# Twenty input loads on ScalarE's queue, w of eight chunks as 64 partitions, transposes by DMA, and a new order

## The chip, the cores and the metric

The kernel runs on one core of a Trainium2 chip. The metric is the device time of one execution in microseconds (us); less is better. Engines are named as in the profile: PE (TensorE), DVE (VectorE), ACT (ScalarE), POOL (GpSimd), SP (SyncE, which here only issues transfers).

## The reference

Two layers in sequence: a recurrent attention with a decaying state, and a gated long convolution.

```python
# r, k, v, w: (4, 8, 768, 48); u: (8, 48)
for t in range(S):
    cur = einsum('bhd,bhe->bhde', u[None] * k[:, :, t], v[:, :, t])
    y[:, :, t] = einsum('bhd,bhde->bhe', r[:, :, t], state + cur)
    state = w[:, :, t, :, None] * state + einsum('bhd,bhe->bhde', k[:, :, t], v[:, :, t])
x = y.transpose(0, 2, 1, 3).reshape(4, 768, 384)
x1, x2, x3 = split(x @ w_proj, 3)                       # w_proj: (384, 1152)
conv = irfft(rfft(x2, axis=1) * rfft(filter_fft, axis=0))  # circular, over 768 steps
out = (x1 * conv * x3) @ w_out                          # (4, 768, 384), float32
```

## The kernel before

**Attention.** The 768 steps of each of 4 batches are cut into 6 chunks of 128, 24 chunks in all (0 to 23). Loads and some elementwise work go by groups of one or two chunks: [0], [1], [2, 3], [4, 5], then pairs. For a chunk i:

- `lw`, `lk`, `lr`, `lv` load 128 tokens x 8 heads x 48 values, one token to a partition. A token's 48 floats of one head lie together in memory, so a packet has 192 bytes (line 1313).
- `ln` takes the logarithm of w; `cs` sums it over time on PE with two triangular masks (lines 1347, 1348) and, in single columns, over the chunk (1350); `ex` takes the exponential on ACT within PSUM (1353); `kq` multiplies it with k and r on DVE (1356); `ph` is the decay of the whole chunk.
- `tr` turns the result on PE, eight 128x128 blocks (1368), and `qk` copies it out of PSUM. `sc` makes the scores (1380), `mt` and `mc` mask them: DVE multiplies with a mask (1396), or ACT copies and POOL cuts (1401).
- `ki`, `kv`, `su` update the state; `yi`, `ys`, `y` make the chunk's output in PSUM; `xn` copies it out, `yt` turns three blocks (1482), `xT` copies them out.
- `rk`, `ru`, `rh`, `cc`, `vc` are the term with u, `vb` is v in bf16.

**Second layer,** for a batch once its chunks are there: `p`, `q`, `xw` are projections (1624, 1661), `cp` and `cxw` copy them out, `cq` multiplies two of them (1649). `sd` folds x2 in time, `f` is the forward transform (1511), `u` and `p` (on DVE) multiply with the filter's spectrum, `E` is the inverse transform (1716). In it the even half is copied out (`cE`), and `aE` add and subtract the odd half (1738, 1742). An `E` marked `Q` in the order works on half the columns, and `dE` make the two halves of the result from it (1751); the others need no `dE`. `yE` multiplies with the gate, `o` is the last projection (1780), `co` copies it out and `so` stores it (1796).

**What sets the order.** Nothing is scheduled at run time. A list of some 1,100 lines, `ORDER`, gives each operation its engine (P, D, A, G or S; M, N, C, Q, V, X are variants of an operation; `-` leaves it out) and, for PE, a PSUM bank; each engine executes its own operations in the list's order and waits by semaphore for what they need. `warm n bank` are n filler matmuls without use (1259). All input loads are issued by SP in the list's order. Input buffers are rotated: w has 3 buffers of a group each, k with r and v have 4, outputs 5 (`NLW, NLD, NO`).

Of the kernel before, what the change touches and what calls it, by code (L numbers as in the profile page):

```python
# [9 lines left out]
FP32 = mybir.dt.float32  # L10
# [28 lines left out]
NLW, NLD, NG, NF, NS, NX, NO = 3, 4, 3, 4, 3, 3, 5  # L39
# [5 lines left out]
warm 16 0  # L45
pads D
smalls D
zeros D
lw0 S
first A  # L50
ln0 A
imaps G
maske G smalls
maps G smalls
ang2 D
ang1 D
lw3 S
lw2 S
lr0 S
lk0 S  # L60
kz2 G
maskn G
cs0 P 4
kz0 G
ln2 A
u S
signs D
maski G
ia1.0 G
ex0 A  # L70
kq0 D
ia2.0 D
warm 9 1
cs3 P 6
kz3 G zeros
cs2 P 2
ur A
warm 5 1
um P 0
rk0 G  # L80
ub A
lv0 S
lw1 S
lr3 S
lk1 S
tr0 P 1
qk0 D
ph0 A
vb0 A
ex3 A  # L90
ln1 A
ang0 D
ru0 G ia2.0
rh0 G kq0
cc0 D
kz1 D
vc0 D
warm 6 0
sc0 P 0
warm 2 4  # L100
cs1 P 4
mt0.1 -
mt0.0 N
kv0 P 0
ex2 A
ex1 A
ia0.0 G zeros
su0 D
mc0.0 C cc0
lk3 S  # L110
lr1 S
mc0.1 -
warm 4 1
yi0 P 0
kq3 D
y0 P
xn0 A
tr3 P 1
kq1 D
lk2 S  # L120
lr2 S
lv1 S
lw4 S
lw5 S
tr1 P 0
rk1 G
ru1 D
rh1 G ru1
ph1 A
qk3 D  # L130
xa0 -
ph3 A
kq2 D
lv2 S
lv3 S
yt0 P 6
sc3 P 4
xT0 A
mt3.0 M
qk1 A  # L140
vb1 A
ph2 A
warm 4 7
tr2 P 6
lr4 S
lk4 S
ki1 P 1
sc1 P 2
qk2 A
mc3.0 -  # L150
mt1.1 -
kv1 P
warm 2 7
sc2 P 6
cc1 D
rk2 G
lk5 S
ru2 D
ia2.1 G
vc1 G  # L160
mc1.1 -
mt1.0 M
mc1.0 -
mt2.1 -
mt3.1 -
lr5 S
ln3 A
warm 5 0
cs4 P 4
yi1 P 2  # L170
rh2 G ru2
su1 D
vb2 G ru2
ys1 P
mc2.1 -
lv5 S
lv4 S
cc2 D
vc2 G cc2
mt2.0 M  # L180
wproj1 G mt2.0
ki2 P 0
y1 P
lw6 S
warm 5 1
kv2 P
xn1 A
ex4 A
cs5 P 2
xa1 -  # L190
mc2.0 -
yt1 P 1
su2 D
ki3 P 0
kv3 P
yi2 P 6
ys2 P
y2 P
mc3.1 -
xT1 A  # L200
kq4 D
tr4 P 1
ex5 A
ph4 A
wproj0 G su2
kq5 D
su3 D
xn2 A
yi3 P 4
ys3 P  # L210
qk4 A
y3 P
rk3 G
xn3 D
warm 4 6
tr5 P 6
qk5 D
xa2 -
ph5 A
yt2 P 2  # L220
lw7 S
xa3 -
yt3 P 7
xT3 D
xT2 D
ki4 P 5
warm 4 1
sc5 P 6
trig A
sin0 A  # L230
sin2 A
vb3 G xn3
mt5.1 -
mc5.1 -
ia1.1 G xT2
kv4 P
sc4 P 3
ia0.1 G xT2
mt4.0 N
ru3 D  # L240
rh3 D
cc3 D
vc3 G cc3
warm 7 1
xw0.2 P 0
is A
mt5.0 M
su4 D
mt4.1 -
xw0.0 P 2  # L250
mc5.0 -
mc4.0 C
yi5 P 6
cxw0.2 D
yi4 P 4
cxw0.0 D
lk7 S
sin1 A
table A
ln4 A  # L260
lr7 S
mc4.1 -
ys5 P
ys4 P
y5 P
xn5 D
y4 P
xn4 D
p0.0.0 P 0
lk6 S  # L270
xa4 -
xa5 -
yt5 P 6
p0.2.0 P 3
lr6 S
rk4 G xn5
xT5 D
yt4 P 2
cs7 P 6
cp0.0.0 D  # L280
filt S
cp0.2.0 D
cs6 P 4
xT4 A
xw0.4 P 0
ex7 A
kq7 D
lv7 S
ex6 A
kq6 D  # L290
cxw0.4 A
if3 A
p0.0.1 P 2
tr7 P 1
ph7 A
cp0.0.1 A
tr6 P 6
qk6 A
qk7 A
sd0.0.0 D  # L300
ru4 D
lw8 S
lw9 S
p0.2.1 P 0
ph6 A
warm 4 7
f0.0 P 2
lv6 S
cp0.2.1 A
cf0.0 A  # L310
sd0.1.0 D
f0.2 P 5
sc7 P 0
mt7.1 -
rh4 D
fsd0 D
fsd1 D
lk8 S
lr9 S
cf0.2 A  # L320
warm 5 7
sc6 P 6
lr8 S
mt7.0 N
mt6.1 -
warm 6 4
h1 P 1
mt6.0 M
ln5 A
cc4 D  # L330
h2 P 4
mc6.0 -
mc7.1 -
lk9 S
mc7.0 C rh4
hc1 A
hg1 D
vb4 G
vc4 G fsd1
lv8 S  # L340
lv9 S
mc6.1 -
lk11 S
hc2 A
h0 P 6
hg2 D
kv6 P 3
su6 D
lk10 S
lw10 S  # L350
lr10 S
hc0 A
cs8 P 0
wproj2 G
warm 2 2
yi6 P 4
y6 P
lw11 S
hg0 D
ex8 A  # L360
xn6 A
xa6 -
yi7 P 2
ys7 P
y7 P
xn7 A
xa7 -
cs9 P 4
kq8 D
lr11 S  # L370
ex9 A
yt6 P 3
yt7 P 7
xT7 D
kq9 D
xT6 A
ki7 P 2
kv7 P
tr8 P 6
qk8 D  # L380
ph8 A
rk5 G cc4
ru5 G
vb5 A
lv11 S
xw1.0 P 0
lr12 S
lv10 S
tr9 P 3
sc8 P 6  # L390
if2 A
ph9 A
lw12 S
rh5 D
cc5 D
lk12 S
lw13 S
lv13 S
cxw1.0 A
qk9 A  # L400
lv12 S
mt8.1 -
su7 D
lk13 S
mt8.0 M
vc5 G cc5
lk15 S
f0.1 P 4
q0.2.0 P 3
ki8 P 2  # L410
cq0.2.0 D
mc8.1 -
sc9 P 0
lr13 S
cf0.1 A
mt9.0 N
mc9.0 C
if1 A
kv8 P
q0.0.1 P 6  # L420
q0.2.1 P 3
yi8 P 4
ln6 A
u10.0 D
mt9.1 -
su8 D
cq0.0.1 D
mc8.0 -
u00.0 D
yi9 P 1  # L430
lw15 S
# [3 lines left out]
lk14 S  # L435
mc9.1 -
xn8 A
lw14 S
lr14 S
xa8 -  # L440
y9 P
lr15 S
q0.0.0 P 6
lv15 S
yt8 P 0
cs10 P 4
if0 A
xn9 A
xa9 -
ki9 P 2  # L450
yt9 P 1
lk17 S
cq0.0.0 D
lv14 S
xT8 A
ex10 A
xT9 A
kv9 P
lw17 S
cs11 P 6  # L460
ex11 A
p1.2.0 P 0
cq0.2.1 D
rk6 G cq0.0.1
cp1.2.0 A
su9 D
lv17 S
ru6 D
xw1.2 P 1
kq10 D  # L470
tr10 P 3
kq11 D
rh6 G ru6
ph10 A
cxw1.2 A
p1.0.0 P 4
cc6 D
p0.0 D
ph11 A
qk10 A  # L480
cp1.0.0 A
ln7 A
tr11 P 7
vb6 G
vc6 G
q1.0.0 P 1
qk11 D
sc10 P 3
sc11 P 6
q1.2.0 P 5  # L490
lr17 S
lw16 S
ki10 P 0
mt10.1 A
cq1.0.0 D
cs12 P 1
mt10.0 D
lk16 S
yi10 - 3
ys10 P  # L500
mt11.1 -
mc11.1 -
mc10.0 -
mc10.1 G
y10 P
mt11.0 N
cs13 P 6
kv10 P
cq1.2.0 D
ex12 A  # L510
xn10 V
kq12 D
vb7 G
ex13 A
E0.0 P 4
mc11.0 C mt10.0
ph12 A
yi11 - 1
cE0.0 A
su10 D  # L520
kq13 D
ph13 A
tr12 P 3
ys11 P
kv12 P 0
aE0.0.0 D
rk7 G
ru7 G
xa10 -
qk12 A  # L530
y11 P
E0.1 P 6
xn11 V
xa11 -
su12 D
cE0.1 A
aE0.0.1 D
dE0.0.0 -
rh7 G aE0.0.0
yt11 P 1  # L540
xT11 D
yt10 P 0
ki13 P 3
tr13 P 2
E0.2 P 4
kv13 P
aE0.1.1 D
aE0.1.0 D
xT10 A
qk13 D  # L550
ln8 A
cE0.2 A
sc12 P 6
lk18 S
lr16 S
mt12.1 -
su13 D
aE0.2.1 D
aE0.2.0 D
mt12.0 N  # L560
sc13 P 0
p1.0.1 P 2
mt13.1 D
mt13.0 D
lv16 S
cp1.0.1 A
cs14 P 6
ex14 A
dE0.1.0 -
xw1.4 P 4  # L570
q1.0.1 P 1
cc7 D
kq14 D
cq1.0.1 D
p1.2.1 P 3
vb8 A
cxw1.4 A
rk8 G
# [240 lines left out]
ex22 A
# [1059 lines left out]
```

## Time and profile before

| | |
|---|---|
| median of 3 runs | 155.38 us (154.06 to 155.63) |
| profiled execution | 153.79 us |
| its span, first to last instruction | 152.1 us |
| busy: PE, DVE, ACT, POOL | 142.4, 135.6, 123.1, 96.1 us |
| input loads by SP | 96, of 192 KB each |
| packets, bytes of the hardware queue | 102,498, 24.78 MB |
| filler matmuls | 90 |
| granted TensorE clock | 1.000 |

The profile is of one execution. An engine's busy time is the union of its instructions' times; the rows of single instructions overlap by some tens of nanoseconds, so that the rows of an engine sum to more. A stretch of time can be cut out and each engine's busy time read in it. "Idle before" names what ended an engine's wait. The chain of waits goes back from the last instruction, at each step to what released it.

### The profile page before, as it was taken

The page shows a single profiled execution, that of the slowest core. Times are in us where ns is not written, and L with a number is a line of the kernel's source. Part 1 is how long each engine was busy: PE and PEld are TensorE (multiplying, and loading weights), DVE is VectorE, ACT ScalarE, POOL GpSimd, SP SyncE. Part 2 cuts the span into 40 slices and gives each one's busy share as a digit, 9 for nine tenths or more (in the row PEclk, how much of TensorE's full clock was granted, in tenths as well). Part 3 has the DMA queues.
Part 4 walks back from the last instruction along what each step waited for, and adds up shares of the span by engine and source line. Part 5 has one row for each costly group of instructions (what it writes and reads, how often), then busy time and mean ns, then how long its engine had stood idle before and what let it go on. Part 6 is the DMA issues. An engine that isn't in the chain of part 4 may idle for free.

```text
span 152.1 us, 4409 instructions
## 1 busy us (share of the span) xinstructions
PE 142.4 (94%) x1725; PEld 95.3 (63%) x1725; DVE 135.6 (89%) x252; ACT 123.1 (81%) x204; POOL 96.1 (63%) x101
## 2 busy tenths in 40 slices
PE   7986999999999999999999999999999999999980
PEld 5654667666556657567666776576687666656530
DVE  3589996989969999999989999999999999999950
ACT  4576849989979989997889899979999987576370
POOL 6577989944069567888968974885299164830310
PEclk9999999999999999999999999999999999999999
DMA  4999899999999999989899899998940000002956
GB/s 97 216 214 223 163 221 174 203 182 272 250 209 170 197 172 219 212 162 218 170 203 218 160 203 192 198 213 169 324 133 0 4 0 0 4 0 88 395 210 240
DMA packets 104118, 26.23 MB, mean 172 GB/s; under 512 B 100129, under 2 KB 102690, under 8 KB 104098
## 3 DMA queue, kind: packets, MB, share of 16 engines
q1 hardware_dynamic: 102498, 24.78, 74.2%
q0 software_dynamic: 1600, 1.18, 5.6%
q8 instruction: 13, 0.21, 0.5%
q14 instruction: 7, 0.06, 0.1%
HBM read 22.41 MB, written 4.72 MB: 178 GB/s over the span
## 4 chain that ended last, share of the span: by engine, by line
PE 42%; DVE 15%; DMA 13%; SPq 10%; ACT 8%; issue 5%; POOL 4%; POOLq 1%; DVEq 0%; ACTq 0%
SPq L1313 10%; PE banks L1624 7%; PE banks L1511 6%; PE banks L1780 5%; DMA w<-in_w_dram 5%; PE banks L1661 3%; PE banks L1368 3%; PE banks L1380 3%; DMA v<-in_v_dram 3%; DMA kr<-in_r_dram 3%; DVE kq L1356 3%; PE banks L1458 3%; DMA kr<-in_k_dram 2%; ACT banks L1353 2%; PE banks L1716 2%
## 5 line engine op out<-in xcount | busy, mean ns | idle before, releaser
L1209 POOL TENSOR_TENSOR rk<-kr 128x768 bf16<-128x768 f32 (+1 forms) x13 | 23.0, 1766 | 9.5 <-DMA kr<-in_r_dram 5.9
L1624 PE MATMUL banks<-xT,wproj 128*128 128x384 bf16 x144 | 27.9, 326 | 0.2 <-ACT x L1213 0.2
L1356 DVE TENSOR_TENSOR kq<-banks,kr 128x768 bf16<-128x768 f32 x24 | 22.4, 949 | 3.6 <-DMA kr<-in_k_dram 1.7
L1401 POOL TENSOR_SCALAR_AFFINE_SELECT mt<-mt 128x512 bf16<-128x512 bf16 (+1 forms) x15 | 14.0, 940 | 12.7 <-ACT mt L1213 8.6
L1209 POOL TENSOR_TENSOR vc<-vb,cc 128x768 bf16<-128x768 bf16 (+1 forms) x11 | 17.4, 1577 | 5.1 <-DVE cc L1332 3.3
L1353 ACT ACTIVATE banks<-banks 128x768 f32<-128x768 f32 x24 | 19.1, 806 | 0.5 <-PE banks L1350 0.2
L1624 PEld LDWEIGHTS <-wproj 128*128 128x128 bf16 x144 | 13.0, 97 | 8.1 <-issue 0.7
L1213 ACT ACTIVATE x<-banks 128x768 bf16<-128x768 f32 (+1 forms) x24 | 16.8, 709 | 1.6 <-PE banks L1661 1.1
L1396 DVE TENSOR_TENSOR mt<-banks,mask_excl 128x1024 bf16<-128x1024 f32 (+1 forms) x17 | 16.2, 965 | 0.2 <-PE banks L1380 0.2
L1213 ACT ACTIVATE qk<-banks 128x1024 bf16<-128x1024 bf16 x16 | 16.2, 1029 | 0.0
L1368 PE MATMUL banks<-ident,kq 128*128 128x128 bf16 x192 | 14.3, 219 | 1.4 <-ACT xn L1213 0.6
L1259 PE MATMUL banks<-wt 128*128 128x256 bf16 x90 | 14.4, 300 | 1.1 <-DVE wt L1282 1.1
L1368 PEld LDWEIGHTS <-kq 128*128 128x128 bf16 x192 | 11.8, 97 | 4.2 <-DVE kq L1356 1.6
L1780 PE MATMUL banks<-wout,y 128*128 128x384 bf16 x72 | 13.3, 326 | 0.5 <-DVE g L1649 0.3
L1661 PE MATMUL banks<-wproj,xT 128*128 128x384 bf16 x72 | 13.6, 325 | 0.0
L1511 PE MATMUL banks<-sd,F 128*128 128x384 bf16 (+1 forms) x96 | 13.4, 328 | 0.2 <-ACT phi L1360 0.2
L1319 ACT ACTIVATE lg<-w 128x768 bf16<-128x768 f32 (+1 forms) x13 | 10.4, 799 | 3.4 <-DMA w<-in_w_dram 3.4
L1213 ACT ACTIVATE mt<-banks 128x512 bf16<-128x512 f32 (+1 forms) x15 | 11.6, 802 | 1.1 <-PE banks L1380 0.7
L1213 ACT ACTIVATE o<-banks 128x768 f32<-128x768 f32 (+1 forms) x12 | 9.3, 785 | 3.5 <-PE banks L1780 3.4
L1511 PEld LDWEIGHTS <-F 128*128 128x128 bf16 (+1 forms) x120 | 8.5, 103 | 5.8 <-issue 1.1
L1649 DVE TENSOR_TENSOR g<-banks,x 128x384 bf16<-128x384 f32 (+1 forms) x16 | 11.8, 748 | 0.3 <-PE banks L1624 0.2
L1209 DVE TENSOR_TENSOR U<-X,hh 128x2304 bf16<-128x2304 bf16 (+1 forms) x12 | 11.9, 1022 | 0.0
(109 smaller groups left out, 331.1 us busy)
## 6 DMA issues: line engine op xcount, KB each, us to landing
w<-in_w_dram SPq DMA_DIRECT2D x24, 192.0 KB, 4.4
kr<-in_r_dram SPq DMA_DIRECT2D x24, 192.0 KB, 3.9
kr<-in_k_dram SPq DMA_DIRECT2D x24, 192.0 KB, 3.8
v<-in_v_dram SPq DMA_DIRECT2D x24, 192.0 KB, 3.9
out_dram<-o SPq DMA_DIRECT2D x11, 384.0 KB, 4.0
U<-in_moe_filter_fft_dram SPq DMA_DIRECT2D x1, 1152.0 KB, 7.3
wproj<-in_moe_w_proj_dram POOLq DMA_DIRECT2D x3, 288.0 KB, 5.9
out_dram<-o SPq DMA_DIRECT2D x2, 192.0 KB, 2.2
```

What stands on the lines that cost most here:

```text
L1209: return eng(e).tensor_mul(o, a, b)
L1213: return nc.scalar.activation(out=o, in_=a, func=AF.Copy)
L1259: nc.tensor.matmul(banks[:, at, 0:256], wt[:, 0:L], wt, start=True, stop=True)
L1313: op(f"l{name}{i}", [SP], lambda e, bk, t=t, x=x, q=q, rw=rw: nc.sync.dma_start(out=t[:, q], in_=x[b, :, rw, :].rearrange("h t d -> t h d" ...
L1353: op(f"ex{i}", [ACT], lambda e, bk: nc.scalar.activation(out=two(bk, f"cs{i}")[:, :, 0:C], in_=two(bk, f"cs{i}")[:, :, 0:C], func=AF.Exp), ...
L1356: op(f"kq{i}", [DVE], lambda e, bk: nc.vector.tensor_mul(kq[f][:, :, :, 0:D], two(bk, f"cs{i}")[:, :, 0:C].rearrange("p a (h d) -> p a h d ...
L1368: nc.tensor.transpose(p[:, HP * m + j, :], kq[f][:, m, 2 * j:2 * j + 2, :], ident)
L1396: return copy(ACT, o, x) if e in (ACT, ACT2) else nc.vector.tensor_mul(o, x, _mid(mask_excl, z - HP * a))
L1511: nc.tensor.matmul(p[rows], F[:, ti, c0 + rows.start:c0 + rows.stop], x[q][:, ti, :], start=(ti == 0), stop=(ti == NT - 1),)
L1624: nc.tensor.matmul(p, wproj[:, cb, col0:col0 + L], xT[bx][:, cb, sl], start=(cb == 0), stop=(cb == CB - 1),)
L1661: nc.tensor.matmul(view(bk)[:, z], xT[bx][:, cb, (c0 + z) * L:(c0 + z + 1) * L], wproj[:, cb, C:2 * C], start=(cb == 0), stop=(cb == CB - 1),)
L1780: nc.tensor.matmul(view(bk)[:, z], yt_[:, z, :], wout[:, cb, :], start=(cb == 0), stop=(cb == CB - 1),)
```

## The change

- **Order.** `ORDER` is another list throughout: other places, other engines for many operations, other PSUM banks.
- **Loads on ScalarE.** A load may be issued by ACT. Twenty of the 96 are: lw0, lw3, lr0 ahead of everything else on ACT, then lk3, lr1, lr2, lv2, lw5, lk4, lk6, lv7, lv6, lw12, lk10, lr13, lv12, lv15, lk20, lw20, lv20, each at a place among ACT's operations.
- **w in pairs of tokens.** For groups 2 to 5 (chunks 2 to 9) w is loaded as 64 partitions, each with two tokens that follow one another: 384 bytes lie together, and two chunks fill one tile's 128 partitions. `cs` then multiplies with two half masks for even and odd tokens, and with twice as many one-column matmuls; four small masks are made on POOL.
- **Transposes by DMA.** For the last eight chunks qk and xT may be made by a DMA transpose that SP issues, with no `tr` or `yt` on PE and no copy: qk18 to qk23 and xT17 to xT23, without xT16, 13 in all.
- **Batch 3 folded.** `E3` may work on half the columns like the other folded ones, with `dE3`; it does.
- **Choices that are new:** two buffers `xe` through which the products of `kq`, `cq` and `aE` may go to POOL (two `cq` do, no `kq` and no `aE`); more operations may go to other engines.
- **Buffers and fillers.** Outputs have 4 buffers, `xf` has 1. Filler matmuls are issued two at a time as one of 512 columns; the list has 81 in place of 90.

How many operations have another engine, from the two lists (before, after): masks of scores on DVE in halves 8, 15, and whole 9, 7; qk on ACT 16, 10; xT on ACT 17, 9, on DVE 7, 8; xn on DVE 12, 16, on ACT 10, 7; tr on PE 24, 18; yt on PE 24, 17; dE on DVE 7, 12; yE on DVE 12, 15 and on POOL 3, 0.

The diff without the list, cut:

```diff
-NLW, NLD, NG, NF, NS, NX, NO = 3, 4, 3, 4, 3, 3, 5
+NLW, NLD, NG, NF, NS, NX, NO = 3, 4, 3, 4, 3, 3, 4
+PAIRS = range(2, 6)
+HL = L // 2
+NTURN = 8
+NE = 2
...
-    def warm(n, at):
-        for _ in range(n):
-            nc.tensor.matmul(banks[:, at, 0:256], wt[:, 0:L], wt, start=True, stop=True)
+    def warm(n, at, lo=0):
+        for z in range(0, n, 1 if lo else 2):
+            hi = min(lo + 256, 512) if lo or z + 1 == n else 512
+            x = _mid(wt, 2) if hi - lo == 512 else wt[:, 0:hi - lo]
+            nc.tensor.matmul(banks[:, at, lo:hi], wt[:, 0:L], x, start=True, stop=True)
...
+    def halves(m, cmp, val, q):
+        o = mask_two[m][q * HL:q * HL + HL]
+        return lambda e, bk: nc.gpsimd.affine_select(
+            out=o, in_=o, compare_op=cmp, fill=val, base=0, pattern=[[1, 2], [-1, L]], channel_multiplier=2,
+        )
...
+    def folded(t):
+        return t.rearrange("p a h d -> p (a h d)").rearrange("p (h x) -> p h x", h=H)
+
+    def ring(e):
+        return nc.scalar if e == ACT else nc.sync
...
+            if gi in PAIRS:
+                op(f"lw{i}", [SP, ACT], lambda e, bk, q=q, rw=rw: ring(e).dma_start(
+                    out=folded(wl[sw])[q * HL:q * HL + HL],
+                    in_=w[b, :, rw, :].rearrange("h (p e) d -> p h (e d)", e=2)), w=[f"w.{sw}.{q}"], cost=2)
...
-                op(f"l{name}{i}", [SP], lambda e, bk, t=t, x=x, q=q, rw=rw: nc.sync.dma_start(
+                op(f"l{name}{i}", [SP, ACT], lambda e, bk, t=t, x=x, q=q, rw=rw: ring(e).dma_start(
                     out=t[:, q], in_=x[b, :, rw, :].rearrange("h t d -> t h d")), w=[...])
...
+        def cs_halves(e, bk):
+            p = two(bk, f"cs{i}")
+            at = slice(q * HL, q * HL + HL)
+            for z, m in ((0, "n"), (1, "e")):
+                for par in (0, 1):
+                    nc.tensor.matmul(
+                        p[:, z, 0:C], mask_two[m][at, par, :], lg[fg][at, par, :, 0:D], start=not par, stop=bool(par),
+                    )
+            for j in range(HP):
+                for par in (0, 1):
+                    nc.tensor.matmul(
+                        p[:, 1, C + j:C + j + 1], lg[fg][at, par, 2 * j:2 * j + 2, :], ones[at],
+                        start=not par, stop=bool(par),
+                    )
...
+        def turn_qk(e, bk):
+            if e == SP:
+                return nc.sync.dma_start_transpose(out=qk[f], in_=kq[f].rearrange("p a h d -> p (a h d)"))
+            return copy(e, qk[f].rearrange("p a t -> p (a t)"), one(bk, f"tr{i}").bitcast(BF16))
...
+        def turn_x(e, bk):
+            if e == SP:
+                return nc.sync.dma_start_transpose(out=xT[b % 2][:, :, rows], in_=xn[:, i % NX])
+            return copy(e, xT[b % 2][:, :, rows], turned(bk))
...
                 for m in (1, 0, 2):
-                    op(n if m == 1 else f"{n}.{m}", [PE], part(m, m == 1, m == 2),
+                    op(n if m == 1 else f"{n}.{m}", [PE, FOLD], part(m, m == 1, m == 2),
```

Parts of the new list that the prediction speaks of. On SP, late: `lw22 lw21 lr21 lr20 qk18 lw23 qk19 xT17 lv21 lk22 qk20 lr22 lr23 lv23 lk23 qk21 so0.0 lv22 qk22 xT19 xT18 qk23 xT20 so0.1 xT21 xT23 xT22 so0.2`. On ACT, first: `lw0 lw3 lr0 first ln0 lk3 ln2 ex0 lr1 ph0 ex3`, and last: `cE3.1 cE3.0 cE3.2 co2.1 co2.0 co3.3 co3.2 co3.0 co3.1`.

More of the change, by code (lines that the diff above doesn't have):

```diff
@@ L110 @@
-lk3 S
-lr1 S
+ub D
+imaps G zerop
+ang1 D
+masknp1 G kz0
+maski G
+kz1 G
+lk3 A
+ln2 A
+ex0 A
+ia2.0 G
+ang0 D
+warm 1 0
+cs2 P 3
+kq0 D
+lv0 S
+warm 3 0
+cs3 P 0
+ang2 D
+rk0 D
+ia0.0 G
+ia0.1 G kz0
+lr1 A
+ph0 A
+ex3 A
+kq3 D
+lk1 S
+ln1 A
+vb0 G
+ew3 -
+lr2 A
+ew0 -
+kw0 -
+warm 9 2
+tr0 P 7
+warm 4 2
+cs1 P 5
+ex1 A
+ph3 A
+qk0 D
+ew1 -
+lk2 S
+lv1 S
+ru0 G kq3
+lv4 S
+lv3 S
+warm 1 2
+kv0 P 2
+ex2 A
+kw3 -
+tr3 P 7
+lv2 A
+ew2 -
+lw4 S
+ia1.0 G rk0
+rh0 D
+su0 D
+kq1 D
+cc0 D
+rk1 G
+warm 2 0
@@ L432 @@
+yi9 P 6
+lw17 S
 ys9 P
@@ L1004 @@
-u03.2 D
+lv21 S
+ph21 A
+yi18 - 2
+tr20 - 7
+ew21 -
+kw21 -
+o0.2 P 6
+sd2.1.0 D
+co0.2 A
+sd2.0.0 D
+mc18.0 G u01.0
+mc19.1 -
+lk22 S
+qk20 S
+cs22 P 4
+p1.0 D
+y18 P
+xn18 X
+p2.2.1 P 0
+vb11 G ru11
+lr22 S
+sc20 P 6
+mc19.0 G sd2.0.0
+q2.0.1 P 2
+xq2.0.1 -
+ex22 A
+kq22 D
+rh11 G
+lr23 S
+lv23 S
+mt20.1 -
+mc20.1 -
+mt20.0 N
+ew22 -
+q2.2.1 P 1
+cs23 P 6
+cp2.2.1 A
+lk23 S
+cq2.2.1 -
+ph22 A
+ki20 P 0
+yi19 P 4
+kv20 P
+ys19 P
+y19 P
+cq2.0.1 D
+ex23 A
+ew23 -
+cc11 D
+tr21 - 6
+qk21 S
+su20 D
```

1861 lines of the change are left out of this document (958 added, 903 removed).

## The prediction

> **What bounds the kernel now.** I read the page first (busy rows, slices), then the table of stretches cut where stages change, the groups by form, and last the chain of waits.
>
> ```profile
> PE 142.4 (94%) x1725; PEld 95.3 (63%) x1725; DVE 135.6 (89%) x252; ACT 123.1 (81%) x204; POOL 96.1 (63%) x101
> PEclk9999999999999999999999999999999999999999
> DMA  4999899999999999989899899998940000002956
> q1 hardware_dynamic: 102498, 24.78, 74.2%
> w<-in_w_dram SPq DMA_DIRECT2D x24, 192.0 KB, 4.4
> ```
>
> The clock is full throughout. The DMA engines are full from 4 to about 112 us: the loads of all 24 chunks, in packets of 192 bytes, fill that time. They then rest until the stores at the end.
>
> ```profile
> core 0: us, PE busy (x) PEld busy (x) DVE busy (x) ACT busy (x) POOL busy (x), PEclk, DMA share, GB/s
> 0.00:7.68 7.68, 6.57 (x47) 4.66 (x48) 3.26 (x28) 3.79 (x5) 4.58 (x22) 1.00 0.80 156
> 7.68:50.00 42.32, 39.13 (x520) 26.48 (x517) 37.63 (x62) 35.38 (x57) 29.97 (x29) 1.00 1.05 207
> 50.00:90.00 40.00, 39.43 (x544) 26.83 (x544) 38.37 (x65) 36.08 (x64) 31.39 (x23) 1.00 1.00 194
> 90.00:146.00 56.00, 55.49 (x611) 36.44 (x610) 55.60 (x99) 45.84 (x78) 30.14 (x28) 1.00 0.50 124
> 146.00:152.10 6.10, 1.76 (x11) 0.85 (x9) 0.73 (x2) 2.00 (x3) 0.00 (x0) 1.00 0.68 258
> ```
>
> The DVE column matters most. From its first large operation (kq0 at 7.68 us) on, DVE idles 4.69, 1.63 and 0.40 us in the three middle stretches, 6.7 us together; 4.42 lie before and 5.37 at the end. PE looks as full, but its ends are modelled and its count holds 90 filler matmuls. The chain of waits is made of loads up to 76.8 us, of PE up to 131, of DVE after:
>
> ```profile
> 72.13 4.55 DMA v<-in_v_dram
> 120.39 0.98 PE banks L1661 x6
> 136.58 2.81 DVE U L1209 x6
> ```
>
> So input, PE and DVE are in balance, and a change helps only where it helps all three. DVE has the least room, so I make the sum on DVE.
>
> **DVE's work.** I counted its operations in both orders and priced each by its form's row (busy over count).
>
> ```profile
> L1396 DVE TENSOR_TENSOR mt<-banks,mask_excl 128x1024 bf16<-128x1024 f32 x9 | 10.9, 1216 | 0.2 <-PE banks L1380 0.2
> L1396 DVE TENSOR_TENSOR mt<-banks,mask_excl 128x512 bf16<-128x512 f32 x8 | 5.3, 682 | 0.0
> L1751 DVE TENSOR_TENSOR y<-y 128x384 bf16<-128x384 bf16 x7 | 2.1, 352 | 0.0
> L1649 DVE TENSOR_TENSOR g<-banks,x 128x768 bf16<-128x768 f32 x8 | 7.6, 949 | 0.0
> ```
>
> More: 7 half masks (0.66 each, 4.6), 4 xn (2.1), 1 xT (0.3), 5 dE (1.5) and 3 yE (1.1), mostly because batch 3 is now folded too, cf0.1 (0.95), and small ones (ur, ub, zerop, kz, sd: 1.7). Two that DVE does not do before are bounded: rk0 between 0.35 (384 elements in bf16) and 0.55 (from f32), if1 likewise; I take 0.45 each. Sum +13.1. Less: 2 whole masks (2.4), 2 products cq (1.5), 2 copies cp (1.1), cxw0.2 (0.95), 2 rh and 2 ru (1.9), vc, hg1, co3.1, an angle (2.4). Sum -10.3. Net +2.8 us of rows. Rows overlap: DVE's rows sum to 148.7 against 135.6 busy, so each counts 0.91.
>
> By stage, up to the same operation in both orders: before kq0 +1.4, from kq0 to kq12 (67.6 us) +3.2, to kq23 (112.3 us) -2.8, after it +1.0. The first part lies in the 4.42 us in which DVE waits for k0 and costs nothing; uncovered it would be 1.3. The rest is +1.4 x 0.91 = **+1.3 us**.
>
> **The loads.** The 102,498 packets of q1 took 74.2% of 16 engines over 152.1 us, 17.6 ns each; a load of 1024 packets is 1.13 us of all engines. Eight w loads now have 512 packets of 384 bytes. No load here has that size: if a packet costs the same, a load saves 0.56; if it goes by bytes, nothing; writing to 64 partitions might even lose as much. A line from 17.6 ns through the stores (3072 bytes at some 400 GB/s, 124 ns) gives 25 ns, 0.34 saved, 2.7 us in all by chunk 9. DVE can use it only where it waits for a load: between kq0 and kq12 the trace has one such wait, 1.3 us for in_r. I take **-1.3**; none is the one end, all 5.4 us idle there the other. At the start two queues issue, and w3 and w2 are shorter: k0, fifth in line, could land about 1 us earlier, but ex0 on ScalarE now follows three issues, a table load and lk3. I take **-0.5**, between 0 and -1.
>
> **ScalarE.** Its rows lose 10.9 us (6 qk 6.1, 8 xT 3.9, smaller ones both ways). It gains 20 issues. ScalarE issued none before; SP's took 0.4 us at least and about 1.0 on the mean while the rings are full, 3.9 at most. Twelve lie between ex0 and ex12. Behind each stand, in order, exps, copies of PSUM banks and state decays, for which PE and DVE wait. Room to that point: some 9 us idle before, plus 4.9 of removed work, 13.9. At 1.0 each the twelve take 12: covered, at no cost, but nearly without reserve. SP is freed of 20 issues of 0.8 to 1.0, which brings no data sooner while the DMA share is 1.00. The Trainium skill, "DMA: Bandwidth & Descriptors", section "Issuing engines are not separate DMA queues", says that issuing from several engines saves only the sequencer's time; by it the 20 issues gain nothing, as counted here.
>
> **PE.** Six qk turns (8 matmuls, 0.55) and seven xT turns (3, 0.21) go to DMA: -4.8. Folding batch 3 halves twelve matmuls: -1.0. Fillers 90 to 81: -1.1. Eight cs with two half masks need two more matmuls of 0.165 and four one-column ones: 0.43 becomes 0.90, +3.7, early, where loads and DVE rule. After kq12 PE gets about 6 us lighter but DVE only 1.7: DVE sets the end there, so PE's relief counts 0. GpSimd adds four small masks (0.4 each) at 63% busy: 0.
>
> **The 13 transposes on SP.** Not seen before. Nearest rows: stores of 192 KB land in 2.2 us, loads in 3.8. Until chunk 18's scores DVE does kq19 and five more, 3.6 us; until sd3.0.2 after xn22, about 4.2. By the rows they fit: **0**; at 6 us they cost 2 to 4. Behind a transpose that waits for its kq or xn, SP holds lk22, lr22, lr23, lv23, lk23; kq22 comes 6.5 us after kq20, enough for 3.8.
>
> **The end.** Output buffers go from 5 to 4: co3.2 now waits for the store of o2.1, which starts only after cE3.2. Along the rows (0.8 copy, 0.4 issue, 3.2 to landing) it comes **0.4** late, between 0 and 1.3, and co3.0 and co3.1 stand behind it on ScalarE.
>
> **Sum:** 152.1 + 1.3 - 1.3 - 0.5 + 0.4 = 152.0 us of span. The profiled execution took 153.79 us, 1.7 more than its span, and the median of the runs lies 1.6 above that: 152.0 + 1.7 + 1.6 = **155.3 us**, no change. About 1% (1.5 us) is what a measurement of this kernel can tell.
>
> **Rivals.**
> - *The small waits go (faster).* With DMA, PE and ScalarE all lighter, DVE's 6.7 us idle could fall to 2 rather than 5.4: 148.6, so 151.9 us. For it: 90 to 146 us shows DVE running with 0.4 idle in 56. Against: most of the idle time lies before 67 us, where DVE gets 3 us more work and ScalarE twelve issues.
> - *ScalarE's issues block it (slower).* Place: ex0 to ex12. It decides once an issue takes over 13.9/12 = 1.16 us; at 1.5 they take 18, 4.1 over: 156.1, so 159.4 us. For it: SP's medians of 0.75 to 0.9 with tails to 3.9, under full rings. Against: a second queue that is mostly empty may issue at 0.4.
> - *The transposes are slow.* At 6 us, sc18 is 2.4 late and sd3.0.2 1.8, and loads of 22 and 23 slip: 155 to 156, so about 159 us. The Trainium skill, "VectorE: DVE Perf Modes", section "The three transpose paths", gives 1309 ns for one 128x128 block by DMA; a qk has eight, an estimate of 10.5 us if one follows another, which no run here shows.
> - *The change does not do what it says:* 384-byte packets take twice the time. Then 1.3 is lost, 156.6 us, within the forecast's own range.
>
> **Chances.** Level 0.42 (own range 153 to 157.5: within 1% 0.22, faster 0.13, slower 0.07); small waits go 0.24; ScalarE blocks 0.19; slow transposes 0.15, of these two 0.03 ending within 1%. Faster 0.13 + 0.24 = 0.37, same 0.25, slower 0.38. The range goes from the faster rival with 1 us of idle left and the start's full 1 us (151.9 - 1.0 - 0.5 = 150.4) to the two slower ones in part together (159.4 + 2.1 = 161.5).
>
> **What would show it.** Right: DVE busy near 138, idle between kq0 and 146 us near 5.4, kq0 near 7.2, the eight w loads at half the packets and landing sooner, the chain late on DVE. Wrong: ScalarE's queue among the chain's largest shares or issues over 1.2 us (second rival), qk or xT by DMA as releaser of PE (third), DVE idle below 3 us (first).

## Result and the profile after

The changed kernel is level with the kernel before to within 1.5%, and by three of four comparisons a little slower. It was measured four times against runs of before on the same chip. Executions more than 1.5% above the fastest of their kernel are left out of every ratio in this document, though not of the medians, and the traces of e1, e2, e3, e3b, d1, d2, p1, p2b and p3b are of such executions.

| occasion | median after, before | ratio, 95% interval |
|---|---|---|
| the first result | 155.61, 154.72 us | 1.0145 [1.01, 1.0191] |
| c_same | 156.64, 156.96 us | 0.9961 [0.9919, 1.0002] |
| c_again | 156.70, 156.15 us | 1.0069 [1.003, 1.0108] |
| c_beside | 157.32, 156.83 us | 1.0064 [1.0018, 1.011] |

The mean of the four ratios is 1.006. The intervals of the first two do not overlap, so an interval from one occasion is too narrow.

The profiled execution after took 155.39 us, with a span of 153.7 us against 152.1. Of its page, the lines that answer to those of before, with the second hardware queue and the DMA transposes (columns as there):

```profile
PE 143.3 (93%) x1660; PEld 89.9 (58%) x1660; DVE 136.7 (89%) x265; ACT 114.6 (75%) x188; POOL 94.9 (62%) x103
PEclk9999996599999999999999999999999999999999
DMA  4999999997999699998999999999999633901175
q1 hardware_dynamic: 87874, 23.11, 73.6%
q10 hardware_dynamic: 19776, 3.93, 14.1%
...
w<-in_w_dram SPq DMA_DIRECT2D x19, 192.0 KB, 5.7
...
xT<-xn SPq DMA_TRANSPOSE x7, 2.3
qk<-kq SPq DMA_TRANSPOSE x6, 3.9
```

ScalarE lost 8.5 us of work and DVE gained 1.1. The clock, full throughout before, is at half for two slices. A load of w on SP's queue lands in 5.7 us at the median, not 4.4. The table of stretches, cut at the same places but for the first and the last end:

```profile
0.00:8.07 8.07, 6.96 (x32) 2.74 (x32) 5.00 (x35) 3.44 (x4) 6.36 (x27) 1.00 0.87 165
8.07:50.00 41.93, 39.00 (x470) 25.06 (x468) 35.93 (x58) 28.18 (x46) 25.13 (x26) 0.92 1.17 213
50.00:90.00 40.00, 39.66 (x545) 26.88 (x544) 38.35 (x64) 35.84 (x62) 30.79 (x26) 1.00 1.06 192
90.00:146.00 56.00, 54.42 (x605) 33.65 (x602) 55.24 (x104) 44.38 (x74) 32.65 (x28) 1.00 0.73 154
```

Only the second stretch is clearly worse: DVE idles 6.0 us in 41.9 (4.7 in 42.3 before), and the clock averages 0.92. Cut instead at the same operations of DVE in both traces, as the prediction did (DVE's busy time in brackets):

| stretch | before | after | change | predicted |
|---|---|---|---|---|
| start to kq0 | 7.68 (3.26) | 8.07 (5.00) | +0.39 | -0.5 |
| kq0 to kq12 | 59.94 (54.61) | 64.17 (57.20) | +4.23 | +1.6 |
| kq12 to kq23 | 44.68 (43.54) | 41.31 (40.50) | -3.37 | -2.5 |
| kq23 to the end of the last `yE` | 33.87 (33.61) | 34.68 (34.02) | +0.81 | +0.9 |
| from there to the end | 5.93 (0.56) | 5.47 (0.00) | -0.46 | +0.4 |
| span | 152.1 | 153.7 | +1.60 | -0.1 |

The loss is ahead of kq12: 2.6 us there are DVE's additional work, which the prediction has (2.9), and 1.6 are additional idle time. DVE's largest single wait there is 2.05 us, of kq5 for r5. The chain of waits around it (start, length, what):

```profile
9.94 5.88 DMA v<-in_v_dram
15.86 6.56 DMA w<-in_w_dram
...
23.33 0.81 PE banks L1512 x4
...
24.39 1.16 PE banks L1512 x3
```

Ahead of chunk 4 the chain is made of two loads in succession: vb1 on ScalarE waits for v1, lw5 stands behind vb1 in ScalarE's order and is issued only at 15.86 us, and most of its cs follow at half the clock.

### The profile page after: what moved, and what is told of

It is laid out like the page before. It is cut to its first block, busy times and chain, and to the rows that moved or that the text cites. A ratio compares the mean times of both kernels' runs of the same rounds, so it can differ in the third digit from the quotient of the medians.

```text
span 153.7 us, 4292 instructions
## 1 busy us (share of the span) xinstructions
PE 143.3 (93%) x1660; PEld 89.9 (58%) x1660; DVE 136.7 (89%) x265; ACT 114.6 (75%) x188; POOL 94.9 (62%) x103
## 4 chain that ended last, share of the span: by engine, by line
PE 32%; DMA 23%; DVE 22%; ACT 9%; SPq 7%; issue 3%; POOL 1%; ACTq 0%; DVEq 0%; POOLq 0%
DMA w<-in_w_dram 8%; PE banks L1816 6%; SPq L1467 6%; DMA qk<-kq 6%; DVE U L1334 5%; PE banks L1996 5%; DMA kr<-in_k_dram 4%; DMA v<-in_v_dram 4%; PE banks L1857 3%; PE banks L1549 2%; PE banks L1512 2%; PE banks L1645 2%; DMA kr<-in_r_dram 2%; DVE kq L1334 2%; ACT X L1338 2%
## 5 line engine op out<-in xcount | busy, mean ns | idle before, releaser
L1334 POOL TENSOR_TENSOR rk<-kr 128x768 bf16<-128x768 f32 (+1 forms) x12 | 21.8, 1813 | 4.4 <-DMA kr<-in_r_dram 2.2
L1338 ACT ACTIVATE x<-banks 128x768 bf16<-128x768 f32 (+1 forms) x27 | 18.4, 690 | 6.0 <-PE banks L1857 3.8
L1583 DVE TENSOR_TENSOR mt<-banks,mask_excl 128x512 bf16<-128x512 f32 (+1 forms) x22 | 18.4, 853 | 0.8 <-PE banks L1567 0.6
L1588 POOL TENSOR_SCALAR_AFFINE_SELECT mt<-mt 128x512 bf16<-128x512 bf16 (+1 forms) x13 | 12.4, 950 | 8.4 <-ACT X L1338 3.1
L1386 PE MATMUL banks<-wt 128*128 128x512 bf16 (+2 forms) x48 | 14.3, 404 | 1.1 <-DVE wt L1424 1.1
L1338 ACT ACTIVATE mt<-banks 128x512 bf16<-128x512 f32 (+1 forms) x13 | 10.1, 794 | 3.0 <-DMA w<-in_w_dram 2.1
L1549 PE MATMUL banks<-ident,kq 128*128 128x128 bf16 x144 | 11.6, 228 | 0.3 <-DVE kq L1334 0.2
L1484 POOL TENSOR_TENSOR rk<-rk 128x384 bf16<-128x384 bf16 (+1 forms) x9 | 8.2, 909 | 5.4 <-DVE rk L1334 4.2
L1340 POOL CAST vb<-v 128x768 bf16<-128x768 f32 (+1 forms) x7 | 6.2, 884 | 7.4 <-PE banks L1567 3.9
L1549 PEld LDWEIGHTS <-kq 128*128 128x128 bf16 x144 | 9.3, 103 | 2.4 <-DVE kq L1334 1.3
```

The costliest lines, as they stand in the source:

```text
L1334: return eng(e).tensor_mul(o, a, b)
L1338: return nc.scalar.activation(out=o, in_=a, func=AF.Copy)
L1386: nc.tensor.matmul(banks[:, at, lo:hi], wt[:, 0:L], x, start=True, stop=True)
L1549: nc.tensor.transpose(p[:, HP * m + j, :], kq[f][:, m, 2 * j:2 * j + 2, :], ident)
L1583: return copy(ACT, o, x) if e in (ACT, ACT2) else nc.vector.tensor_mul(o, x, _mid(mask_excl, z - HP * a))
L1588: return nc.gpsimd.affine_select(out=o, in_=o, pattern=[[0, z - HP * a], [1, L]], compare_op=ALU.is_gt, fill=0.0, base=0, channel_multipli ...
```

## Experiments

My theory after this was that the loads late for kq5 and the half clock cost what the change gains elsewhere; the rivals were that ScalarE's issues, the pairs or the transposes are themselves the cost. The theory fell in its second half. Its first half stands, but why the loads are late is settled only in part; it is taken up under wproj below.

**ScalarE's twenty loads back to SP** (every `lX A` to `lX S` at its place; e1_all_sp), and only the eleven later ones (lk6 to lv20; e5_late_sp):

```diff
-lv6 A
+lv6 S
```

> The twenty ScalarE loads are issued by SP again, each at its old place in the list; all else as in the changed kernel (profiled span 153.7 us). Theory A (hardware transfers share eight completion semaphores, counted over both queues in the list's order, so ScalarE stands still until somebody else's transfer has landed, and SP until ScalarE has issued; this is what makes the stretch up to chunk 12 late): kq12 comes 1.5 to 3 us earlier than 72.2, ScalarE's waits for transfers shrink, span 151 to 152.5. Rival B (the loads are late because the 16 DMA engines are full and the list asks for them in another order; who issues does not matter): kq12 within 0.7 us of 72.2, span 153 to 154.5. Rival C (SP becomes the limit when it issues all): kq12 later, span 155 or more.

> The changed kernel with the eleven later of ScalarE's loads (lk6 to lv20) back on SP at the same places, the nine early ones (lw0 to lk4) left on ScalarE. All twenty on SP cost 4.6% of the kernel before, against a changed kernel within 1.5% of it. If the early part of the list rests on two queues, this is within 1% of the changed kernel; if it is the stretch with the transposes, where SP stands, it is 2 to 4% slower and kq up to 12 stay where they were.

Measured: 163.97 us, 1.0461 [1.0341, 1.058], and 164.74 us, 1.0613 [1.0426, 1.0801]. Both are far above the changed kernel. In e1 kq12 comes at 79.3 us, as its rival C had it. e5 is beyond either of its expectations. In e5, kq6 and kq7 are at 40.1 and 41.4 us as in the changed kernel, but kq8 at 60.1 instead of 53.8. From the waits of e5 between 38 and 62 us (who waited for what: us, times, longest):

```profile
POOL vb L1340 <- DMA v<-in_v_dram: 9.2, 1, 9.2
```

In e5's chain the load that vb4 waits for, lv6, starts at 46.83 us; in the trace of c_same ScalarE issued it at 42.41. So the edit does not only change who issues: in the list lv6 stands behind five loads of SP, three of which it overtook on ScalarE's queue. What the second queue is worth in this place is that a load need not stand behind others that wait.

**What a load and a transpose cost by themselves** (m1_loads).

```diff
+    for i in range(16): plain(nc.sync, ...)
+    for i in range(16): pairs(nc.sync, ...)
+    for i in range(16): plain(nc.scalar if i % 2 else nc.sync, ...)
```

> No kernel of the layers: sixteen loads of w of 192 KB by SP in packets of 192 bytes, then sixteen in pairs of tokens (384 bytes, 64 partitions each), then sixteen in packets of 192 bytes issued by SP and ScalarE in turn, then six DMA transposes of 128x1024, then four stores; the whole computation is left out. If a packet has its price whatever its size, a paired load takes 0.56 us of the sixteen engines where a plain one takes 1.13, and the second stage takes half as long as the first (9 us against 18). If the price goes by bytes, both stages take the same. By the prediction's line, the second takes 0.7 of the first. A second queue shortens the third stage only if one queue does not fill the engines: on the row of the changed kernel (218 GB/s against 212 in the kernel before at 4 to 12 us), by no more than 5%. The transposes: 2 to 4 us each to landing, some 1.2 to 2.3 us apart as SP issued them.

DVE reads one value of every second load when it has landed. From DVE's timeline (start, us, line, operation, and the idle time before), one read from the middle of each stage:

```profile
11.96 0.15 DVE L71 COPY seen<-w 128x1 f32<-128x1 f32 x1 [1.63 <-DMA w<-in_w_dram]
...
31.52 0.15 DVE L71 COPY seen<-pr 128x1 f32<-128x1 f32 x1 [1.47 <-DMA pr<-in_w_dram]
...
47.04 0.15 DVE L71 COPY seen<-mx 128x1 f32<-128x1 f32 x1 [1.65 <-DMA mx<-in_w_dram]
```

The read before each of them began at 10.17, 29.89 and 45.23 us. So two plain loads take 1.79 us, two paired ones 1.63, two plain ones from two queues 1.81. A paired load saves 0.08 us, about a tenth, where the prediction's line had 0.34; the second queue adds no bandwidth. It does change how long a load is on its way. From the page, the plain loads of the first and of the third stage, with the median time from issue to landing at the end of the line:

```profile
w<-in_w_dram SPq DMA_DIRECT2D x16, 192.0 KB, 3.8
...
mx<-in_w_dram SPq DMA_DIRECT2D x8, 192.0 KB, 6.5
mx<-in_w_dram ACTq DMA_DIRECT2D x8, 192.0 KB, 6.5
```

With two queues a load takes 6.5 us to land instead of 3.8, at the same rate. At 0.9 us a load, seven are then under way at once, not four. That is no loss by itself, but a landing time read with one queue can't be taken over to two.

The page has the rates as bytes: its GB/s row stands mostly at 216 to 223 in the first and third stage and at 238 to 258 in the second. The Trainium skill, "DMA: Bandwidth & Descriptors", section "Why small descriptors are slow (HBM only)", counts some 3 cycles of overhead per packet beside one per 32 bytes; that estimate (15 cycles for 384 bytes against 18 for two of 192) gives 0.83, where 1.63 over 1.79 is 0.91: the direction is right, the gain half of it.

SP issued the six transposes in 8.21 us, 1.4 us each; they landed in 3.3 us at the median. That is close to the prediction's value for a qk (3.8) and far from the rival's 10.5.

**The pairs.** Undone in the changed kernel (e2_no_pairs), and alone in the order of before (p1_pairs):

```diff
-PAIRS = range(2, 6)
+PAIRS = range(0)
```

> w of chunks 2 to 9 is loaded one token to a partition again, with the plain cs; the small masks are still made, the list is the same. If paired w loads save 0.34 us of all engines each, as predicted, then without them the loads of chunks 4 to 9 come 1 to 2.5 us later and the span is 1 to 3 us longer (154.7 to 156.7). If they save nothing: within 0.7 us of 153.7. If they cost something (64 partitions, and 0.47 us more PE work for each cs): shorter, 151 to 153.

> The kernel before with one part of the change: w of chunks 2 to 9 as pairs of tokens, with the halved masks and the additional cs matmuls, in the order of before (four small masks and one zeroing added at the start). Theory A (loads arrive at a nearly fixed number of bytes per microsecond; the sixteen loads alone gave 242 GB/s in pairs against 217, so eight w loads save 0.8 us in all): by the time of kq5 four of them have saved 0.4 us, and the ratio to before is 0.995 to 1.01, the additional PE work included. Theory B, the prediction's own term (0.34 us per load, 1.3 us at the end): 0.98 to 0.995.

Measured: undone 160.90 us, 1.0203 [1.0062, 1.0343]; alone 156.96 us (155.54 to 161.53), 1.0025 [0.9985, 1.0065]. Alone they bring nothing that can be told, as theory A has it. Undone the middle value is about a per cent and a half above the changed kernel, more than the 0.6 us of transfer that eight times 0.08 allow, but it rests on two runs, and the interval goes down to the changed kernel's own mean of 1.006; in that trace the clock is at half from 25 to 32 us and again near 100, with an average of 0.962. Part of what the halved masks do here may be to keep PE busy; that was not separated.

**The half clock** (e4_fill): three groups of fillers ahead of kv1, kv3 and cs4, the places where PE waited.

```diff
+warm 8 6
 kv1 P
...
+warm 6 0
 kv3 P
+warm 8 3
 cs4 P 0
```

> Three more groups of filler matmuls (8, 6 and 8 of 256 columns) where PE waits at 15, 20 and 22 us, ahead of kv1, kv3 and cs4; all else as in the changed kernel. Theory of the clock (PE's pauses between 14 and 24 us are followed by a granted clock of 0.5 from 24 to 31 us, and that costs time): clock 1.0 throughout or nearly, chunk 12 and the span 1.5 to 3 us earlier (150.7 to 152.2). Rival (the half clock only fills time in which loads are waited for, kq5 waits 2.0 us for in_r with or without it): clock 1.0, span within 0.7 us of 153.7.

> The changed kernel once more, so that the two rearrangements of its order stand beside it on one chip. It was 1.0145 times the kernel before; both theories expect 1.01 to 1.02 here, and the granted clock at half speed for some 6 us about 25 us into the span, as in its first profile.

From the stretches of 2 us, the changed kernel first, then e4 (PE's busy time is the first number behind the comma, the clock the third from the end):

```profile
20.00:22.00 2.00, 1.30 (x26) 0.78 (x26) 1.54 (x4) 0.65 (x1) 1.75 (x2) 1.00 1.00 179
22.00:24.00 2.00, 1.21 (x22) 0.82 (x20) 1.93 (x5) 1.94 (x4) 1.29 (x3) 1.00 0.97 168
24.00:26.00 2.00, 2.00 (x22) 1.10 (x21) 1.95 (x2) 1.00 (x3) 2.00 (x3) 0.51 1.21 173
...
28.00:30.00 2.00, 2.00 (x33) 1.58 (x28) 1.80 (x4) 0.80 (x2) 1.76 (x1) 0.50 1.26 207
```

```profile
28.00:30.00 2.00, 2.00 (x49) 1.67 (x50) 2.00 (x5) 1.39 (x5) 1.40 (x2) 1.00 1.25 255
```

The fillers keep the clock: its mean is 0.997, and 0.994 or more in eight of e4's ten runs, against 0.967 to 0.985 in c_same's twelve. The time does not follow: 156.86 us, 1.0009 [0.9957, 1.0061], between the ratios of the changed kernel itself, of which c_same, at 0.9961, had been expected at 1.01 or more. kq12 comes at 71.2 us rather than 72.2, but kq23 at 114.0 rather than 113.5. So the half clock is real, but no gain from removing it could be measured; as the main cause it falls.

**The loads for kq5** (d1_loads), and both edits together (d2_both):

```diff
-lv4 S
...
+lw5 A
 vb1 A
...
-lw5 A
...
-lv5 S
...
 lr5 S
+lv4 S
+lv5 S
```

> The changed kernel with three of its loads at other places: lv4 and lv5 behind lr5 on SP, and lw5 ahead of vb1 on ScalarE. Theory A (the loads arrive at a fixed number of bytes per microsecond, so that what the list puts ahead of r5 sets when kq5 runs): kq5 waits for in_r 2.05 us in the changed kernel; two loads fewer ahead of it, of 0.9 us each at the 217 GB/s seen, take 1.8 of it away, and 0.5 to 1.5 us of that is left at the end, 0.3 to 1% of the time. Theory B (the half clock at 24 to 31 us is what costs): kq4 and kq5 still wait, now for the exponentials behind slow cs, and the time does not move by more than 0.3 us unless the clock comes back.

> The three loads moved as above and three groups of fillers on PE as in the earlier run (ahead of kv1, kv3 and cs4). If the late loads and the half clock are two causes, their gains add: kq8 comes at 51 to 52 us rather than 53.8 and the time is 1.0 to 2.5 us below the changed kernel's. If they are one cause, it is no faster than the better of the two edits alone.

d1 is slower than the kernel before: 159.46 us, 1.0126 [1.0046, 1.0206]. For d2 there is no ratio; its six runs go from 154.79 to 159.40 us. In its trace kq8 comes at 55.4 us, not at the 51 to 52 of two gains that add. kq5's wait is gone in d1 (kq4 and kq5 follow each other from 24.25 us on; kq5 of before starts at 24.32), but kq6 comes at 42.6 us, later than in the changed kernel (39.8). vb3 now waits for its loads of v, the two that I had moved back, and PE for vb3 (the waits from 22 to 44 us):

```profile
PE banks L1608 <- POOL vb L1340: 5.0, 1, 5.0
...
POOL vb L1340 <- DMA v<-in_v_dram: 4.7, 1, 4.7
```

The list puts lv4 and lv5 ahead of r5 for a reason, then. What can make a load of this stretch so late is the matter of the next part.

**wproj in the same stretch.** GpSimd issues two loads of 288 KB (wproj1, wproj0) at 21 to 24 us, on a queue of its own, and vb3 reads two loads of v that SP issues at the same time. Over all traces with the order of before, from the timelines of SP and GpSimd, with kq6 from DVE's (in us):

| trace | second v issued | wproj issued | vb3 starts | kq6 |
|---|---|---|---|---|
| before | 21.85 | 22.69 | 26.34, no wait | 35.5 |
| p3_start | 21.61 | 22.83 | 26.41, no wait | 35.5 |
| p3_again | 21.81 | 22.82 | 26.40, no wait | 35.4 |
| p3b_start | 22.19 | 23.23 | 26.81, no wait | 36.5 |
| p2b_turn | 22.49 | 22.71 | 30.15, waited 3.5 | 41.4 |
| p2_turn | 22.87 | 22.92 | 30.38, waited 3.6 | 40.5 |
| p1_pairs | 23.30 | 23.28 | 32.01, waited 4.4 | 43.2 |

They differ in this stretch only by p1's pairs and the loads that p3 starts with. With 0.84 us or more ahead of wproj the v load is there in time; with 0.22 or less it takes over 7 us, and kq6 comes 5 to 8 us late. It is not the late issue alone: p3b's v is issued later than before's, but so is its wproj, and vb3 does not wait. Two of them on GpSimd's timeline, first p3_again, then p2_turn:

```profile
22.82 1.79 POOL L1434 DMA_DIRECT2D wproj<-in_moe_w_proj_dram  x2
...
26.40 0.83 POOL L1336 CAST vb<-v 128x768 bf16<-128x768 f32 x1
```

```profile
22.92 1.79 POOL L1434 DMA_DIRECT2D wproj<-in_moe_w_proj_dram  x2
...
30.38 0.82 POOL L1336 CAST vb<-v 128x768 bf16<-128x768 f32 x1 [3.58 <-DMA v<-in_v_dram]
```

In the changed kernel wproj1 is issued at 21.02 us, and the load that it meets is r5, issued at 20.59 (19.98 before). It lands 7.5 us later, not 4.2 as before; in this trace that is kq5's wait. From its timelines:

```profile
21.02 0.99 POOL L1438 DMA_DIRECT2D wproj<-in_moe_w_proj_dram  x1
...
28.20 0.96 DVE L1334 TENSOR_TENSOR kq<-banks,kr 128x768 bf16<-128x768 f32 x1 [2.05 <-DMA kr<-in_r_dram]
```

d1 fits too: it moved the v loads behind wproj1 (19.93 there), and vb3 started at 29.49. So a load that goes out half a microsecond later at this place can come some four later. That is read from the traces; a kernel with wproj moved away was not tried.

In the changed kernel wproj can't be all of it. In c_again r5 is issued at 19.86 us, 2.56 ahead of wproj1, and takes 7.1 us to land all the same; kq5 is as late there without waiting for r5:

```profile
28.71 0.96 DVE L1334 TENSOR_TENSOR kq<-banks,kr 128x768 bf16<-128x768 f32 x1 [0.52 <-ACT banks L1530]
```

kq5 starts at 28.36 us in c_same and at 27.87 in c_beside, with waits of 0.33 and 0.70 us; before it is 24.32. And loads that go out well ahead of wproj are slow as well. Of SP's issues between 12 and 20 us, before first, then the changed kernel:

```profile
v<-in_v_dram SPq DMA_DIRECT2D x3, 192.0 KB, 3.7
```

```profile
v<-in_v_dram SPq DMA_DIRECT2D x3, 192.0 KB, 6.2
```

The w5 of the chain above is another: 6.56 us, and it has landed at 22.42, before a packet of wproj moves. In that stretch both hardware queues are at work, as in m1's third stage, where 6.5 us stood against 3.8. What lies at the second queue and what at wproj in the changed kernel was not separated.

**The transposes.** Undone in the changed kernel at the list's own places (e3_turn_pe), undone at places 8 to 16 lines ahead of their use (e3b_turn_pe), and alone in the order of before (p2_turn, p2b_turn):

```diff
-tr18 - 3
-qk18 S
+tr18 P 4
+qk18 D
```

> The 13 transposes by DMA go back to PE with a copy by ScalarE (6 qk, 7 xT); all else as in the changed kernel. If the transposes cost nothing, as predicted, and PE and ScalarE had room: same, within 0.7 us of 153.7. If they are waited for (the chain shows 8.6 us of qk by DMA): 1 to 3 us shorter. If they were worth their relief of 4.8 us PE and 10 us ScalarE after chunk 18: 1 to 3 us longer, with DVE idle between 90 and 146 us above 1.5.

> The changed kernel with the 13 transposes back on PE and copies on ScalarE and DVE in turn, now each at a place 8 to 16 lines ahead of its use rather than where the list had its skipped line (there PE stood for kq and the run said nothing of the transposes). If the DMA transposes are worth what the prediction said (0, PE and ScalarE being no limit there), this is 1.00 to 1.02 times the changed kernel; if PE and ScalarE would limit without them, 1.03 to 1.06, with DVE waiting for ScalarE's copies between kq18 and kq23.

> The kernel before with another part: qk18 to qk23 and xT17 to xT23 turned by DMA transposes of SP at the places of the copies they replace, nothing else moved. Theory A (the transposes take work from PE and ScalarE, which are not the limit in that stretch, and delay what stands behind them on SP and wait for them): 1.00 to 1.03. Theory B (PE and ScalarE are the limit after chunk 17, as the far worse time of the changed kernel without transposes would have it): 0.97 to 0.99.

> The kernel before with the 13 DMA transposes alone, as in the earlier run, but without the four small masks that had been put ahead of wout on GpSimd there (they made wout wait, and the projection waited 4.0 us for it). Theory A (the transposes block SP, and what stands behind them, where they wait for their kq or xn): 1.02 to 1.05, the loss between kq18 and kq23. Theory B (nearly all of the earlier loss was wout): 0.99 to 1.01.

| run | median | ratio, interval |
|---|---|---|
| e3_turn_pe | 178.40 us | none; before 156.78 |
| e3b_turn_pe | 168.56 us | 1.0798 [1.0434, 1.1162] |
| p2_turn | 166.94 us | 1.0695 [1.0624, 1.0766] |
| p2b_turn | 165.11 us | 1.0577 [1.0247, 1.0907] |

e3 says nothing of the transposes: PE met them where the list only had a skipped line, and stood 5.1 us at once for a kq. p2 had an error of mine: the four small masks that it does not need stood ahead of wout on GpSimd, and the projection waited 4.0 us for it. Without that (p2b) it is still 6% slower. Of the 11.6 us by which kq23 is late in p2b's trace (123.9 against 112.3), 5.3 are there at kq18 already, before any transpose: that is the late v load of the table. The other 6.3 come with the transposes. SP stands from 92.6 to 97.8 us at that of chunk 18, with loads behind it, and PE waits for an xT (waits from 84 to 135 us):

```profile
PEld L1853 <- DMA xT<-xn: 5.9, 2, 5.0
...
PE banks L1853 <- DMA xT<-xn: 5.1, 2, 4.6
```

This is the prediction's third rival in the old order: loads stand behind a transpose on SP, and PE waits for an xT by DMA. In the new order the same 13 transposes are nearly hidden: the chain has 8.6 us of them from 113.69 us on, but DVE idles only 0.76 us between 90 and 146. Put back on PE there, turns and copies cost some 7% against the changed kernel (1.0798 over 1.006, from two runs), of which 5.0 us are DVE's own work, since half of the copies went to it (141.7 us busy, not 136.7); DVE's idle time is the larger rest. Each order goes with one way of turning.

**The start** (p3_start, p3b_start, p3_again): the order of before with lw0, lw3 and lr0 on ScalarE ahead of everything there. In p3_start the masks stood ahead of wout as in p2; it is told for completeness.

```diff
+lw0 A
+lw3 A
+lr0 A
 first A
```

> The kernel before with a third part: lw0, lw3 and lr0 issued by ScalarE ahead of everything else there, the rest of the order as before. The prediction's term for the start is 0.5 us earlier for kq0 (0.3% of the time: 0.997). Theory A (two queues share one rate: 218 GB/s from two against 217 from one in the loads alone): k0 is issued earlier but the first packets land no sooner, kq0 within 0.3 us of 7.7 us, ratio 0.997 to 1.005. Theory B (the queue's place matters): kq0 before 7.2 us.

> The kernel before with lw0, lw3 and lr0 on ScalarE alone, again without the masks ahead of wout, for which the projection had waited 2.7 us at 99 us. Up to 88 us the earlier run lay within 0.4 us of the kernel before at every kq but the first, which was 0.7 us late. Theory A: 0.997 to 1.004, nothing left of the start. Theory B, the prediction's term: 0.997 or less.

> The kernel before with lw0, lw3 and lr0 on ScalarE, once more. It was 0.995 [0.9902, 0.9997] of the kernel before. If the start on two queues is worth the 0.5 us of the prediction's term, 0.994 to 0.998 again; if that was the chance of one occasion, 0.999 to 1.005.

Measured: 1.0118 [1.0041, 1.0195] with the misplaced masks, then 0.995 [0.9902, 0.9997] and 0.9902 [0.9856, 0.9947]; the last at 154.38 us beside 156.83 of before and 157.32 of the changed kernel (c_beside, 1.0064) on one chip. This is the fastest version of all. kq0 comes later in it, not earlier, at 8.4 us against 7.7, and waits for r0, which is issued third on ScalarE; from DVE's timeline of p3b_start:

```profile
8.43 0.96 DVE L1330 TENSOR_TENSOR kq<-banks,kr 128x768 bf16<-128x768 f32 x1 [2.43 <-DMA kr<-in_r_dram]
```

By kq5 it has caught up (24.0 us against 24.3), and from there the trace of p3_again runs with that of before to within 0.4 us; its span is 152.4. The one trace of before is of a run below its median, so a comparison of traces can't show where the runs gain. What the table above lets one suppose, though it is not shown: with the first loads on two queues the second v goes out some 1.0 to 1.2 us ahead of wproj rather than 0.84, and fewer runs fall on the late side; nine of p3_again's twelve runs lie between 153.9 and 154.9 us, those of before spread from 155.0 to 159.2. Besides the three loads this kernel has the changed code's filler matmuls of 512 columns and one buffer xf. p1_pairs has these too, at 1.0025, which speaks against them; they were not tried alone.

> The changed kernel a third time, on another occasion. It was 1.0145 times the kernel before in the first comparison (4 runs of each) and 0.9961 in the second (12 against 23). If there is a difference that belongs to the kernels, this lies on the side of one of the two and outside 0.995 to 1.008; if the two are level, it lies within.

> The changed kernel beside it, on the same chip. If both kernels are level and only the start gains, 1.000 to 1.008, above the other; if the changed kernel has more to give than the start, below it.

Both lie where two level kernels should be, on the slow side.

## Why the prediction came out as it did

The forecast was 155.3 us, no change; the median was 155.61. The first comparison has the changed kernel 1.45% slower, with an interval clear of no change; the other three lie between -0.4 and +0.7%. The second rival's threshold was not reached, and the faster rival did not come: DVE idles 8.4 us between kq0 and 146 us, where the prediction had 5.4 and before 6.7. That the number came out so near is luck: in the working several errors cancel.

- **The loads, -1.3: the step that failed.** It came out as 1.6 us more of idle time between kq0 and kq12. Two things in it were wrong. The line gave 0.34 us for a paired load; alone, it saves 0.08, so 0.3 us for the four ahead of kq5. And the term takes it that a load lands as it did before. In the changed kernel it does not: 6.2 us instead of 3.7 for the v loads of SP between 12 and 20 us, and 7.5 instead of 4.2 for r5, for which kq5 waits 2.05 us. m1 shows that a second queue alone makes such a difference, and the old order shows that wproj's 576 KB can; the list moved wproj into the flight of r5, and I never placed its row of the page in time. How the two share the lateness stays open.
- **DVE's work, +1.3: right in rows, too high in time.** Summed from the timelines, DVE's rows change by +1.9, +2.9, -3.1 and +0.9 us up to kq0, kq12, kq23 and the end, where the count had +1.4, +3.2, -2.8 and +1.0. Its busy time changes by +1.7, +2.6, -3.0 and -0.1, so by -0.6 from kq0 on and not by +1.3: a factor of overlap taken from the whole does not hold for a difference of rows. This hid part of what the loads cost.
- **The start, -0.5:** kq0 came 0.4 later. The working had k0 as the load that kq0 waits for; with lr0 on ScalarE it is r0, and in the changed kernel DVE's own small operations last until 7.84 us. The old order with the three loads on ScalarE is 0.5 to 1% faster, but kq0 is late there too, so this is not the term's gain.
- **ScalarE's issues, 0: right.** Each takes 0.37 to 0.43 us in c_same's trace between 34 and 66 us, less than the 1.0 I had from SP. What I did not see is that such an issue can stand still: in the program it waits for an earlier transfer that uses the same completion semaphore, on either queue. One stood 2.1 us on ScalarE that way, lk4 at 21 us, until w4, a load of SP's, had landed.
- **The transposes, 0: right here, and only here.** PE waits for a qk by DMA twice after 84 us, 0.6 us in all; alone in the old order 6.3 us of the trace's loss come with them.
- **PE, 0:** no gain from its relief shows; the halved masks alone in the old order and the half clock cost none that could be measured.
- **The end, +0.4:** it was -0.5; no copy of an output waits for a store in ScalarE's timeline.
- **From span to median, +1.6:** this came from before's profiled run, which lies below its median. After, the median lies 0.2 us above the profiled run. The span was forecast too low by 1.7, this too high by 1.4.

The price of e1, e5, e2 and e3b is not that of their parts. Each takes a part out of an order that was made with it, and each is slower; p1 and p2b put a part alone into the old order, and these gain nothing either. Which of the parts the new order's gain of 3.4 us between kq12 and kq23 comes from can't be told by such runs. It goes with 3.0 us less work on DVE there, which is a matter of the order's choice of engines rather than of loads.

## What to carry to other kernels

Where the DMA engines are full, place every large transfer in time beside the loads it flies with, those of GpSimd's queue too: in the old order, half a microsecond in a load's place went with 4 us of waiting. Do not carry a load's landing time over to a kernel that issues from two queues: the second queue moved no more bytes here, and each load took longer to land. A second issuing engine can be worth something where a load would otherwise stand behind one that waits, and it can stand still itself, with the engine's own work behind it. A part of a change can't be priced by taking it out of an order that was made with it; put it alone into the old order too, and measure on more than one occasion before a per cent is believed.

## What was not expected

- A packet of 384 bytes takes 1.8 times one of 192 (1.63 against 1.79 us for two loads, half the packets): close to a price by bytes.
- The clock fell to half with no long pause of PE before it: between 14 and 24 us its longest waits are 0.9, 0.8 and 0.7 us, and it was busy 7.6 of 10 us. The Trainium skill, "TensorE: Matmul & The Clock Gate", section "HAM oscillation — how this bites in real kernels", warns of gaps over about 3.4 us; the trace shows the half clock after scattered gaps that add up to less.
- With both queues active the DMA share goes up and the bytes do not: 1.41 at 218 GB/s in c_same between 8 and 12 us, 1.11 at 220 in before. So a share above 1 is no sign of more work done.
- While wproj's packets fly, throughput falls: in the trace of before from 218 GB/s (22 to 24 us) to 141 (24 to 26) and 186 (26 to 28), and SP's loads of the next microseconds land in 7.0 to 8.1 us instead of some 4.
- One program's ratio differs by 2% between occasions (0.9961 and 1.0145), more than either interval.
